# One fused attention, expert and MLP kernel on one Trainium2 core: maxima and halves of the folded weights taken by quarters, and another order of the whole program

## The chip, the cores and the metric

The kernel runs on one core of a Trainium2 chip. The metric is the device time in microseconds (us) of one execution; the median of three runs stands for a kernel. The engines are TensorE (PE, with its weight load PEld), VectorE (DVE), ScalarE (ACT), GpSimd (POOL) and SyncE (SP, which here only issues DMAs). Each works off its own list of instructions in order, and semaphores hold an instruction until its operands are there.

## The reference

Three stages follow one another, for 4 sequences (B) of 576 rows and 512 channels:

```python
attn = softmax(causal(q @ k.T / 8 + decay(f))) @ v         # 8 heads of 64
x    = attn as (B, 576, 512)
# four experts: attention over all rows, then each row keeps its two best
for e in range(4):
    ye = softmax(causal((x @ wq[e]) @ (x @ wk[e]).T / 8)) @ (x @ wv[e]) @ wo[e]
    out += gate[e] * ye                                    # gate: softmax of the two largest of x @ w_gate
# mixer
h = (out.T @ U @ V).T
u = out + h
result = u + relu(u @ w_ch1) @ w_ch2
```

The weights w_ch1 and w_ch2 arrive as 64-bit floats and are turned into 32-bit ones on the chip. The kernel never forms `u` in 512 channels: it keeps the 256 channels of the four heads, folds `wo` into `w_ch1` (512 x 2048 becomes 256 x 2048, the "folded weights"), and later multiplies by `wo` once for the residual.

## The kernel before

Most products are done as three float16 matmuls: each operand is split into a high half (a scaled copy, on ACT) and a low half (the residue, on DVE or POOL), and `TERMS` (line 46) lists the three products that are kept. A split needs a power-of-two scale, and so the largest absolute value of the whole operand: `absmax` (line 329, a DVE reduction), `pow2` (352, over all partitions by one small PE transpose) and `scales` (371).

For each batch b the program runs eight heads of kind 1, written (1, b, h), the projections of their result (`project`, 901, and `values_gates`, 938), four heads of kind 2, (2, b, e), then `mix` (1215), which makes the two halves `z` of the mixer's input, and the MLP: `hidden` (1291; PE tile `hid`, from z and the folded weights), `relu` (1313; tiles g) and `outputs` (1324; tile `acc`, from g and w2). A head is `scores` (553, tile `sp`, or `acc` for 576 columns), `softmax` (581: row minimum on DVE, exponential on ACT, then halves `P`, turned by a DMA transpose into `pt`; some heads are turned on PE instead, `turn_head`, 648), and `pair_pv` (711, the product with V).

The order of the work is written by a planner that runs while the program is built. Every piece above is a thread (`spawn`, 181) with a number from the table `PR` (45); `run` (210) always takes the thread that could start first by the planner's own costs, with `PEN` (39) times its number added as a handicap: a low number goes first. So one number changed in PR can move instructions everywhere.

What is prepared beside the first batch:

- `prep` (1134) issues the loads of U, V, 16 pieces of w_ch1 and 16 of w_ch2, 512 KB each, on SP's queue into three buffers `wd`. `f64_to_f32` (1050) turns a piece into float32: on ACT a scaled copy and a Sign, on DVE a shift and a shift-or, on POOL or DVE a multiply by the sign. Numbers `fold` and `f64_2` of PR go with the pieces of w_ch1 (tile `x`) and w_ch2 (in place in `w2x`).
- `fold` (1110): eight PE matmuls on one piece x and `wtr`, the turned wo, into `hid`; one ACT copy puts the result into `wfr`. The profile shows the eight float32 matmuls of a fold as 16 rows.
- `wf_scaled` (1173) waits for all 16 folds, gives the space of x and wtr to later tiles (`turn`, 1043), takes eight maxima over `wfr`, one scale, and makes eight pairs of halves, in place, one block further down.
- `w2_scaled` (1188) waits for all 16 pieces of w2x, gives the space of `wd` and `sg` to the tiles z and g (line 1190), and makes w2's halves. `w2_done` (1126) takes w2's maxima on ACT or DVE as the planner finds cheaper.
- `hidden` waits once for all halves (event "wf") and then, per batch, for z.

Of the kernel before, what the change touches and what calls it, by code (L numbers as in the profile page):

```python
# [35 lines left out]
WHOLE = 10  # L36
QUEUE = ('act', 'act', 'sp', 'act')
ACTDMA = 100
PEN = 13.823999999999998
WINDOW = 10240 / 3  # L40
WARM = 3300.0
LAG = 100.0
AHEAD = 16
PROJ_EXP = 15
PR = {'load': 3.25, 'low0': -2.0, 'low': 5.75, 'zeros': -2.0, 'scores': 3.25, 'soft0': 1, 'soft2_0': 1.0, 'soft': 5.5, 'soft2_': 9.5, 'pv0': -0.25, 'pv': -0.75, 'pvout0': 2.5, 'pvout': 4.0, 'project0': 3.75, 'project': 0.25, 'vg0': 0.25, 'vg': 4.75, 'out0': 1.75, 'out': 3.0, 'values0': 1.0, 'values': -1.0, 'wall': 5.25, 'prep': 6.0, 'f64': -1.25, 'f64_2': 4.25, 'fold': 2.25, 'wf': 1.25, 'w2': 3.75, 'mix': 0.25, 'relu': 0.75, 'store': 2.75, 'hidden': 6.25, 'outputs': 9.25}
TERMS = ((0, 0), (0, 1), (1, 0))

TURN = {(1, 0): 4, (2, 0): 2}
# [110 lines left out]
class Plan:  # L159
# [21 lines left out]
    def spawn(self, gen, prio=1, t=None):  # L181
        self.seq += 1
        th = {"gen": gen, "t": self.now() if t is None else t, "prio": prio, "seq": self.seq, "last": None}
        self.threads.append(th)
        self.step(th, None)
# [58 lines left out]
def attn_moe_mixer(ctx: ExitStack, tc: tile.TileContext, qk, v, f, wall, wot, wo, w1, w2, u3, v3, out):  # L244
# [7 lines left out]
    spawn = plan.spawn  # L252
# [8 lines left out]
    def mm(out_, lhsT, rhs, start, stop, rate=0.4167, **kw):  # L261
        nc.tensor.matmul(out_, lhsT=lhsT, rhs=rhs, start=start, stop=stop, **kw)  # L262
        small = lhsT.shape[0] <= 64 or size(lhsT) <= 64
        plan.tensor(size(rhs) * rate + 2.5 + (105 if small else 0), size(rhs) * (4 if rate > 1 else 1))
# [48 lines left out]
    def copy_scaled(out_, in_, scale=1.0):  # L313
        act(out_, in_, ACT.Copy, scale=scale)
# [146 lines left out]
    def ev(*name):  # L461
        if name not in E_:
            E_[name] = Event(plan)
        return E_[name]

    def count(n, *name):
        e = ev(*name)
        if name not in counted:
            counted.add(name)
            e.n = n  # L470
        return e
# [571 lines left out]
    def turn(i, *rings):  # L1043

        raw[i].release()
        late = ctx.enter_context(tc.tile_pool(name=f"late{i}", bufs=1, side=SIDES[i]))
        for r in rings:
            r.pool = late
# [61 lines left out]
    def fold(x, c):  # L1110
        yield ev("wtr")
        r = r_hid
        both = yield r
        pp = both[:, :, :128]
        for m in range(2):
            yield "pe"
            for kc in range(4):
                mm(pp[:, m, :], wtr[:, kc, m * 128:(m + 1) * 128], x[:, kc, :], kc == 0, kc == 3, rate=1.8)
        r_x.free(x)
        yield "act"  # L1120
        o = 128 * (c % 4)
        copy_scaled(wfr[:, 1 + c // 4:6 + c // 4:4, o:o + 128], pp)
        r.free(both)
        count(16, "fold").done()

    def w2_done(x, s, c):
        if (yield Any(act=280 + 0.833 * DM, dve=70 + 1.04 * DM)) == "act":
# [6 lines left out]
    def prep():  # L1134
        todo = [(u3.rearrange("p k (n t) -> p k n t", t=2), [128, KB, 96], None, u_done)]
        for c in range(2):
            cs = slice(c * 288, c * 288 + 288)
            todo.append((v3[:, c * 576:(c + 1) * 576].rearrange("p (n t) -> p n t", t=2), [96, 288], None,
                         lambda x, _, cs=cs: v_done(x, cs)))
        ones = [(w1[:, :, c * 256:(c + 1) * 256].rearrange("p k (n t) -> p k n t", t=2), [128, 4, 128], None,  # L1140
                 lambda x, _, c=c: fold(x, c)) for c in range(16)]
        twos = [(w2[:, c, :].rearrange("p (n t) -> p n t", t=2), [128, DM], w2x[:, c + 1, :],
                 lambda x, s, c=c: w2_done(x, s, c), c < 6) for c in [*range(6, NF), *range(6)]]
        todo += ones[:AHEAD]
        for c in range(16):
            todo += ones[AHEAD + c:AHEAD + c + 1] + twos[c:c + 1]
        yield "sp"
        got = dma(wtr, wot)
        spawn(wo_scale(got), PR['prep'])
        yield ev("rows of first")  # L1150
        for src, shape, d, done, *late in todo:
            if len(shape) == 3 and shape[0] == 128 and shape[1] == 4:
                yield ev("aug", 0)
            if d is not None:

                yield ev("aug", B - 1)
                if late[0]:
                    yield ev("wall")
            w = yield r_wd.of(shape + [2], I32, "wd")
            yield QUEUE[2]  # L1160
            spawn(f64_to_f32(w, dma(w, src, queue(2)), shape, d, done), PR['f64' if d is None else 'f64_2'])
# [8 lines left out]
        s_wo[0], _ = scales("won", e, 11)  # L1170
        ev("wo scale").done()

    def wf_scaled():
        yield count(16, "fold")
        yield ev("u")
        yield count(2, "v")
        turn(1, r_ynz, r_th, r_o)
        for i in range(8):
            yield "dve"
            absmax(mxf[:, i:i + 1], wfr[:, 1 + i])  # L1180
        e = yield from pow2("wf", mxf, 8)
        s_wf[0], s_wf[1] = scales("wf", e, 2)
        ev("wf scale").done()
        for i in range(8):
            yield from split(wfs[:, i, 0], wfs[:, i, 1], wfr[:, 1 + i], s_wf[0])
        ev("wf").done()

    def w2_scaled():
        yield count(NF, "w2x")
# [99 lines left out]
    groups = [(b, g) for b in range(B) for g in range((64 * b + 576) // 256)]  # L1289

    def hidden():
        yield ev("wf")
        for b, g in groups:
            yield ev("z", b)
            zt, z0 = ZT[b], g * 256
            for n in range(8):
                r = r_hid if b < B - 1 else r_sp
                hp = yield r.of([128, 2, 256], F32, "hid")
                for fi in range(2):
                    f_ = 2 * n + fi  # L1300
                    fs = slice(f_ % 4 * 128, f_ % 4 * 128 + 128)
                    yield "pe"
                    for kc in range(2):
                        for i, (w_, x_) in enumerate(TERMS):
                            mm(hp[:, fi, :], wfs[:, 4 * kc + f_ // 4, w_, fs], zt[x_][:, kc, z0:z0 + 256], kc + i == 0,
                               kc == 1 and i == 2)
                spawn(relu((b, g, n), r, hp), PR['relu'])
            if (b, g + 1) not in groups:
                count(3 if b < B - 1 else 2, "z free", b).done()
# [163 lines left out]
    spawn(values(0), PR['values0'])  # L1473
    spawn(prep_wall(), PR['wall'])
    spawn(prep(), PR['prep'])
    for b in range(B):
        for p in range(4):
            spawn(pair_pv(1, b, p), PR['pv0' if b == 0 else 'pv'])
        spawn(project(b), PR['project0' if b == 0 else 'project'])
        spawn(values_gates(b), PR['vg0' if b == 0 else 'vg'])  # L1480
        spawn(free_xt(b), 0)
        for p in range(2):
            spawn(pair_pv(2, b, p), PR['pv0' if b == 0 else 'pv'])
        spawn(mix(b), PR['mix'])
        spawn(free_z(b), 0)
# [51 lines left out]
```

## Time and profile before

| | us |
|---|---|
| median of three runs (800.39 to 806.13) | 800.57 |
| the profiled execution | 796.3 |
| its span, first to last instruction | 794.6 |

The profile is of one execution. Its span is 1.7 us shorter than that execution's own time, and that execution is 4.3 us under the median of the runs. The rows that the prediction reads stand in a section of their own below.

### The profile page before, as it was taken

Reading aid. Unit: us, or ns where it says so; the run is one execution under the profiler, and the core shown is the slowest. Engines: PE = TensorE matmul, PEld = TensorE weight load, DVE = VectorE, ACT = ScalarE, POOL = GpSimd, SP = SyncE. Lnnn points to the kernel's source line nnn. Section 1 sums busy time; section 2 is a strip of 40 time slices with the busy share of each in tenths; the row PEclk is TensorE's granted clock in tenths of the full one; section 3 lists DMA queues with packets and bytes.
Section 4 is the critical chain, followed back from the end, with each engine's and each line's share of the span. In section 5 each row is a group of like instructions: output and inputs, shape, how many; then the busy total and the mean of one; then the engine's idle time right before and its main releaser. Section 6 shows DMA issues by size and latency. Waiting matters only on the chain.

```text
span 794.6 us, 15708 instructions
## 1 busy us (share of the span) xinstructions
PE 684.1 (86%) x5720; PEld 480.7 (60%) x5720; DVE 485.6 (61%) x1559; ACT 429.3 (54%) x893; POOL 302.9 (38%) x365
## 2 busy tenths in 40 slices
PE   3777889898655889989969989997999999899996
PEld 2555668686644556756646667565666756555653
DVE  5798985568688884566686637657663572311111
ACT  3677775767586674555656536566562562211121
POOL 4132263234585542247676304666761242000000
PEclk9899999898556999999979999999899999999999
DMA  8546198476589755599999848999976565000000
GB/s 223 128 92 135 45 203 198 136 195 163 144 194 195 135 97 102 109 188 178 221 227 204 134 94 156 179 227 216 199 135 105 121 123 92 27 1 27 1 27 26
DMA packets 210817, 107.28 MB, mean 135 GB/s; under 512 B 172340, under 2 KB 191796, under 8 KB 210708
## 3 DMA queue, kind: packets, MB, share of 16 engines
q1 hardware_dynamic: 190324, 81.28, 52.0%
q0 software_dynamic: 8096, 16.22, 10.3%
q10 hardware_dynamic: 12320, 8.78, 4.8%
q8 instruction: 45, 0.74, 0.4%
q14 instruction: 32, 0.26, 0.1%
HBM read 51.90 MB, written 5.16 MB: 72 GB/s over the span
## 4 chain that ended last, share of the span: by engine, by line
PE 53%; DVE 17%; DMA 12%; ACT 9%; issue 5%; POOL 2%; ACTq 1%; SPq 0%; POOLq 0%; DVEq 0%
PE mm L262 19%; PE acc L262 15%; PE hid L262 12%; DMA pt<-P 10%; PE sp L262 5%; ACT sc L267 3%; DVE sc L273 2%; DVE cols L273 2%; DVE w2x L273 2%; ACT P L267 1%; POOL P L285 1%; DVE pt L273 1%; PE hid L664 1%; DMA YW<-in_qk 1%; ACT pt L267 1%
## 5 line engine op out<-in xcount | busy, mean ns | idle before, releaser
L262 PE MATMUL acc<-w2x,g 128*128 128x512 f16 x768 | 181.4, 381 | 0.0
L285 POOL TENSOR_TENSOR P<-sc,P 128x448 f16<-128x448 f32 (+4 forms) x128 | 102.9, 811 | 149.3 <-ACT P L267 123.6
L262 PEld LDWEIGHTS <-g 128*128 128x128 f16 x864 | 82.3, 98 | 83.7 <-issue 1.9
L267 ACT ACTIVATE sc<-sc,nm 128x576 f32<-128x576 f32 (+4 forms) x195 | 105.7, 558 | 42.9 <-DVE nm L273 40.2
L262 PE MATMUL hid<-z,wfr 128*128 128x256 f16 x864 | 115.5, 283 | 12.8 <-DVE g L273 4.3
L273 DVE SCALAR_TENSOR_TENSOR g<-hid,g 128x512 f16<-128x512 f32 x72 | 49.6, 690 | 119.8 <-ACT g L267 119.7
L262 PEld LDWEIGHTS <-wfr 128*128 128x128 f16 x864 | 84.5, 101 | 39.6 <-issue 11.0
L267 ACT ACTIVATE g<-hid 128x512 f16<-128x512 f32 x72 | 42.6, 592 | 104.9 <-PE acc L262 71.1
L262 PE MATMUL mm<-V,pt 128*128 128x65 f16 (+1 forms) x1992 | 87.4, 205 | 7.7 <-DMA pt<-P 7.1
L267 ACT ACTIVATE P<-sc 64x64 f16<-64x64 f32 (+4 forms) x174 | 74.3, 459 | 30.4 <-DMA pt<-P 27.3
L262 PE MATMUL sp<-X 128*128 128x256 f32 (+1 forms) x132 | 54.5, 420 | 26.1 <-POOL X L285 11.9
L262 PEld LDWEIGHTS <-pt 128*128 128x128 f16 x1872 | 63.1, 99 | 10.1 <-DMA pt<-P 7.6
L273 DVE TENSOR_TENSOR P<-sc,P 128x448 f16<-128x448 f32 (+4 forms) x52 | 42.1, 812 | 25.1 <-ACT P L267 24.6
L262 PEld LDWEIGHTS sp<-X 128*128 128x128 f32 x132 | 29.0, 219 | 40.1 <-DVE nm L273 20.6
L273 DVE CUSTOM_DVE_ANT_0 sc<-sp,mask 128x288 f32<-128x288 f32 (+4 forms) x115 | 48.4, 425 | 7.7 <-POOL P L285 2.9
L285 POOL TENSOR_TENSOR xh<-xn,xh 128x320 f16<-128x320 f32 x30 | 26.6, 888 | 66.3 <-ACT xh L267 65.6
L285 POOL TENSOR_TENSOR x<-x,sg 128x512 f32<-128x512 f32 (+2 forms) x19 | 24.1, 1269 | 71.1 <-ACT sc L267 25.1
L262 PE MATMUL mm<-xt,wall 128*128 128x288 f16 x384 | 51.0, 290 | 0.0
L262 PE MATMUL sp<-Y 68*128 68x256 f32 (+1 forms) x132 | 44.3, 342 | 0.0
L262 PEld LDWEIGHTS <-wall 128*128 128x128 f16 x384 | 38.1, 100 | 9.8
L273 DVE CUSTOM_DVE_ANT_0 sc<-sp,mask,cols 128x192 f32<-128x192 f32 (+4 forms) x80 | 38.1, 487 | 8.9 <-POOL P L285 3.7
L262 PE MATMUL hid<-x,wtr 128*128 128x128 f32 x256 | 35.2, 292 | 2.8 <-POOL xh L285 1.7
(150 smaller groups left out, 1204.0 us busy)
## 6 DMA issues: line engine op xcount, KB each, us to landing
wd<-in_w SPq DMA_DIRECT2D x32, 512.0 KB
Y<-in_qk POOLq DMA_DIRECT2D x22, 288.0 KB, 4.8
R<-in_qk SPq DMA_DIRECT2D x22, 288.0 KB
X<-in_qk POOLq DMA_DIRECT2D x22, 288.0 KB, 5.3
vr<-in_v ACTq DMA_DIRECT2D x16, 320.0 KB
out_dram<-o SPq DMA_DIRECT2D x18, 256.0 KB
Xh<-stg SPq DMA_DIRECT2D x16, 216.0 KB
X<-in_qk POOLq DMA_DIRECT2D x22, 144.0 KB, 4.4
```

The source lines that it names most:

```text
L262: nc.tensor.matmul(out_, lhsT=lhsT, rhs=rhs, start=start, stop=stop, **kw)
L267: nc.scalar.activation(out_, in_, fn, **kw)
L273: getattr(nc.vector, op)(**kw)
L285: getattr(nc.gpsimd, op)(out=out_, **kw)
L664: nc.tensor.transpose(flat[:, 128 * i:128 * i + 128], x[:, 128 * kb:128 * kb + 128], identr)
```

## The change

The rows of `wfr` are laid out by quarters of the 2048 hidden channels (both blocks of 128 input channels of a quarter side by side). The maxima of a quarter wait only for its four folds ("folds", q), the halves report each quarter by itself ("wf", q), and `hidden` waits for the quarter that it uses. The scale is still one for all eight blocks, so every pair of halves stands behind all eight maxima. The release of space is split off into `raw_free`, a thread of its own. Most of the numbers in PR are different, and PEN is a quarter larger; of those that belong to the weights, `fold` goes from 2.25 to 1.75 and `f64_2` from 4.25 to 5.25, and `project0` from 3.75 to 2.25.

```diff
-PEN = 13.823999999999998
+PEN = 17.279999999999998
...
@@ def fold
-        copy_scaled(wfr[:, 1 + c // 4:6 + c // 4:4, o:o + 128], pp)
+        copy_scaled(wfr[:, 1 + 2 * (c // 4):3 + 2 * (c // 4), o:o + 128], pp)
         r.free(both)
         count(16, "fold").done()
+        count(4, "folds", c // 4).done()
...
-    def wf_scaled():
+    def raw_free():
         yield count(16, "fold")
         yield ev("u")
         yield count(2, "v")
         turn(1, r_ynz, r_th, r_o)
+
+    def wf_scaled():
         for i in range(8):
+            yield count(4, "folds", i // 2)
             yield "dve"
             absmax(mxf[:, i:i + 1], wfr[:, 1 + i])
...
         for i in range(8):
             yield from split(wfs[:, i, 0], wfs[:, i, 1], wfr[:, 1 + i], s_wf[0])
-        ev("wf").done()
+            if i % 2:
+                ev("wf", i // 2).done()
...
@@ def hidden
-        yield ev("wf")
         for b, g in groups:
...
             for n in range(8):
+                yield ev("wf", n // 2)
...
-                            mm(hp[:, fi, :], wfs[:, 4 * kc + f_ // 4, w_, fs], zt[x_][:, kc, z0:z0 + 256], kc + i == 0,
+                            mm(hp[:, fi, :], wfs[:, 2 * (f_ // 4) + kc, w_, fs], zt[x_][:, kc, z0:z0 + 256], kc + i == 0,
...
+    spawn(raw_free(), 0)
```

On PE, where the scores of the first heads of kind 2 stand (`Xh`), the program before reads as follows; `hid<-x,wtr` is a fold, in two parts of four matmuls, and `mm<-identr,sc` turns a head on PE.

```order
L262 LDWEIGHTS Xh
L262 MATMUL sp<-Xh 128x448
L262 MATMUL hid<-x,wtr 128x128 x4
L664 MATMUL mm<-identr,sc_96 128x128
L664 MATMUL mm<-identr,sc_97 128x128 x2
L262 MATMUL hid<-x,wtr 128x128 x4
```

At the same scores the changed program reads as follows; `mm<-identr,cols` is the transpose in a scale, here that of the folded weights, and `mm<-wall,xt` belongs to `values_gates`.

```order
L262 MATMUL mm<-wall_81,xt 128x260
L262 MATMUL mm<-identr,cols 128x128
L664 MATMUL hid<-identr,sc_98 128x128 x3
L262 LDWEIGHTS Xh
L262 MATMUL sp<-Xh 128x448
```

Before, 11 of the 16 folds and 66 of the 96 projection matmuls (`mm<-xt,wall`) of batch 0 stand in front of the first scores with Xh; now all 16 and all 96 do.

On DVE, the maxima of wfr stand before among the scores of the last two heads of kind 2 (`sc<-sp,mask,cols`; `ISA nm` reads out a minimum) and right in front of conversions of w2.

```order
L273 TENSOR_REDUCE cols<-wfr 128x1
L273 ISA sc_100,nm<-sp,mask,nm,cols 128x288
L273 ISA nm 128x1
L273 TENSOR_REDUCE cols<-wfr 128x1
L273 TENSOR_SCALAR w2x<-w2x 128x512
L273 TENSOR_REDUCE cols<-cols 128x1
L273 TENSOR_TENSOR rr<-rr,wq 128x5 x2
L273 SCALAR_TENSOR_TENSOR w2x<-wd,w2x 128x512
```

The first two maxima now stand among the conversions of w_ch1 (x), while the last heads of kind 1 of the first nine are still scored.

```order
L273 ISA sp,nm<-sp,mask 128x448
L273 ISA nm 128x1
L273 TENSOR_REDUCE cols<-wfr 128x1
L273 TENSOR_SCALAR x<-x 128x512
L273 TENSOR_REDUCE cols<-wfr 128x1
L273 SCALAR_TENSOR_TENSOR x<-wd,x 128x512
L273 TENSOR_SCALAR nm<-nm 128x1
L273 ISA acc,nm<-acc,mask 128x288
L273 ISA nm 128x1
```

The other six follow in pairs, all in front of the first score of kind 2.

On DVE, the low halves of wfr stand before between conversions of w2 and heads of batch 1.

```order
L273 SCALAR_TENSOR_TENSOR wfr<-wfr,cols 128x512
L273 TENSOR_TENSOR xn<-mm,rr 128x320
L273 TENSOR_SCALAR w2x<-w2x 128x512
L273 TENSOR_SCALAR nm<-nm 128x1 x2
L273 SCALAR_TENSOR_TENSOR wfr<-wfr,cols 128x512
L273 SCALAR_TENSOR_TENSOR w2x<-wd,w2x 128x512
L273 TENSOR_SCALAR w2x<-w2x 128x512
L273 SCALAR_TENSOR_TENSOR wfr<-wfr,cols 128x512
```

They now stand among the scores of kind 2, in front of the gates.

```order
L273 ISA sc_96,nm<-sp,mask,cols 64x64
L273 ISA nm 64x1
L273 ISA sc_97,nm<-sp,mask,cols 128x192
L273 ISA nm 128x1
L273 SCALAR_TENSOR_TENSOR wfr<-wfr,cols 128x512
L273 SCALAR_TENSOR_TENSOR w2x<-wd,w2x 128x512
L273 ISA sc_98,nm<-sp,mask,cols 128x320
```

All eight are now in front of the gates, and four conversions of w2 stand ahead of the last of them; before, they began after the gates had been used, with eight conversions of w2 ahead of the first of them and eleven ahead of the last. Between the use of the gates (`rr<-rr,wq`) and the halves of z, DVE's row holds 11 conversions of w2 and all eight low halves before, and 9 conversions and no half now.

## Rows read from the trace of the kernel before

**Rows 1.** The page, part 1: busy us (share of the span) xinstructions of each engine.
```profile
span 794.6 us, 15708 instructions
...
PE 684.1 (86%) x5720; PEld 480.7 (60%) x5720; DVE 485.6 (61%) x1559; ACT 429.3 (54%) x893; POOL 302.9 (38%) x365
```

**Rows 2.** Windows: stretch, length, each engine's busy us (instructions), PE clock, DMA share, GB/s.
```profile
72.00:94.60 22.60, 16.80 (x156) 11.84 (x156) 20.04 (x67) 16.00 (x33) 3.64 (x4) 0.92 0.42 85
94.60:140.30 45.70, 40.31 (x443) 35.78 (x443) 32.52 (x90) 30.85 (x68) 23.46 (x24) 0.96 0.82 184
140.30:191.80 51.50, 45.16 (x330) 36.47 (x328) 33.76 (x103) 36.61 (x82) 15.13 (x15) 0.93 0.62 165
191.80:255.70 63.90, 40.12 (x235) 35.14 (x235) 52.55 (x127) 44.47 (x96) 41.24 (x43) 0.55 0.78 174
255.70:316.10 60.40, 52.22 (x443) 33.74 (x441) 44.58 (x117) 37.98 (x73) 25.66 (x26) 0.94 0.61 117
316.10:682.00 365.90, 340.10 (x3153) 234.17 (x3153) 226.50 (x852) 198.83 (x425) 173.35 (x211) 0.97 0.88 158
682.00:794.60 112.60, 103.39 (x612) 60.67 (x612) 19.03 (x33) 20.58 (x33) 0.00 (x0) 0.97 0.05 19
```

**Rows 3.** PE's timeline, 70 to 330 us: start, us, line, out<-in, count, [idle before].
```profile
98.23 2.03 PE L262 MATMUL hid<-x,wtr 128*128 128x128 f32 x16
...
136.37 1.27 PE L262 MATMUL mm<-xt,wall 128*128 128x288 f16 x9
...
140.25 1.15 PE L262 MATMUL sp<-Xh 128*128 128x64 f16 x8
...
174.77 6.81 PE L262 MATMUL mm<-V,pt 128*128 128x65 f32 x60
...
202.30 6.50 PE L262 MATMUL mm<-V,pt 128*128 128x65 f32 x30
...
222.53 0.58 PE L262 MATMUL sp<-X 128*128 128x256 f32 x1 [10.96 <-POOL X L285]
...
225.38 3.40 PE L262 MATMUL mm<-y,u 128*96 128x256 f16 x15
```

**Rows 4.** DVE's groups by form: count | busy us, mean ns | idle before.
```profile
L273 DVE TENSOR_SCALAR w2x<-w2x 128x512 int32<-128x512 int32 x16 | 13.0, 813 | 3.1 <-ACT w2x L267 3.1
...
L273 DVE SCALAR_TENSOR_TENSOR w2x<-wd,w2x 128x512 int32<-128x512 int32 x16 | 12.0, 747 | 0.3
L273 DVE SCALAR_TENSOR_TENSOR x<-wd,x 128x512 int32<-128x512 int32 x16 | 11.9, 746 | 0.2
...
L273 DVE SCALAR_TENSOR_TENSOR wfr<-wfr,cols 128x512 f16<-128x512 f32 x8 | 8.7, 1085 | 0.5 <-ACT wfr L267 0.5
...
L273 DVE TENSOR_SCALAR x<-x 128x512 int32<-128x512 int32 x16 | 8.0, 500 | 7.6 <-ACT x L267 7.4
...
L273 DVE TENSOR_REDUCE cols<-wfr 128x1 f32<-128x512 f32 x8 | 5.3, 682 | 0.0
```

**Rows 5.** DVE's timeline, 184 to 262 us.
```profile
191.81 0.24 DVE L273 TENSOR_TENSOR rr<-rr,wq 128x5 f32<-128x5 f32 x2
...
224.94 0.89 DVE L273 SCALAR_TENSOR_TENSOR wfr<-wfr,cols 128x512 f16<-128x512 f32 x1
...
237.73 0.16 DVE L273 RECIPROCAL cols<-cols 128x1 f32<-128x1 f32 x1
...
255.74 1.42 DVE L273 SCALAR_TENSOR_TENSOR z<-y,cols,z 128x1152 f16<-128x1152 f32 x1
```

**Rows 6.** ACT's timeline, 222 to 260 us.
```profile
254.16 0.19 ACT L267 ACTIVATION_READ_ACCUMULATOR sg<-w2x 128x1 f32 x1
254.38 1.26 ACT L267 ACTIVATE z<-y,cols 128x1152 f16<-128x1152 f32 x1
```

**Rows 7.** Tile wfr on DVE: ns min/median/max, first and last start us.
```profile
L273 DVE TENSOR_REDUCE cols<-wfr x8: 676/682/687, 177.7 to 190.8; 128x1 f32<-128x512 f32 x8
...
L273 DVE SCALAR_TENSOR_TENSOR wfr<-wfr,cols x8: 745/864/1747, 204.0 to 224.9; 128x512 f16<-128x512 f32 x8
```

More of the change, by code (lines that the diff above doesn't have):

```diff
@@ L44 @@
 PROJ_EXP = 15
-PR = {'load': 3.25, 'low0': -2.0, 'low': 5.75, 'zeros': -2.0, 'scores': 3.25, 'soft0': 1, 'soft2_0': 1.0, 'soft': 5.5, 'soft2_': 9.5, 'pv0': -0.25, 'pv': -0.75, 'pvout0': 2.5, 'pvout': 4.0, 'project0': 3.75, 'project': 0.25, 'vg0': 0.25, 'vg': 4.75, 'out0': 1.75, 'out': 3.0, 'values0': 1.0, 'values': -1.0, 'wall': 5.25, 'prep': 6.0, 'f64': -1.25, 'f64_2': 4.25, 'fold': 2.25, 'wf': 1.25, 'w2': 3.75, 'mix': 0.25, 'relu': 0.75, 'store': 2.75, 'hidden': 6.25, 'outputs': 9.25}
+PR = {'load': 4.25, 'low0': -1.0, 'low': 5.75, 'zeros': -2.0, 'scores': 3.25, 'soft0': 1.5, 'soft2_0': 0.75, 'soft': 5.75, 'soft2_': 9.5, 'pv0': 0.0, 'pv': -1.0, 'pvout0': 2.75, 'pvout': 7.0, 'project0': 2.25, 'project': -2.0, 'vg0': 0.25, 'vg': 5.75, 'out0': 1.5, 'out': 2.0, 'values0': 1.0, 'values': -0.5, 'wall': 5.25, 'prep': 6.0, 'f64': -1.25, 'f64_2': 5.25, 'fold': 1.75, 'wf': 1.25, 'w2': 3.75, 'mix': 0.25, 'relu': -0.25, 'store': 1.0, 'hidden': 4.25, 'outputs': 9.0}
 TERMS = ((0, 0), (0, 1), (1, 0))
```

## The prediction

> **What bounds the kernel now.** Read the page's first part first: PE is busy for 684.1 of 794.6 us [rows 1], so it bounds the kernel wherever it has work. The windows then say where it has none. From 316.1 us, where batch 1's projections begin, PE is busy for 340.1 of 365.9 us and then for 103.4 of 112.6, at a clock of 0.97: there the time is PE's, and its work is the same after the change [rows 2]. Before that the stages differ. From 72 to 94.6 us DVE has 20.0 of 22.6 us; up to 140.3, where folds and projections share PE, PE has 40.3 of 45.7; up to 191.8, the stage of the heads of kind 2, PE has 45.2 of 51.5 and DVE only 33.8. Then comes the poor stage, 191.8 to 255.7: PE is busy for 40.1 of 63.9 us and that at a granted clock of 0.55, thus almost wholly at 1.2 GHz, while DVE has 52.6, ACT 44.5 and POOL 41.2 us [rows 2]. No engine is full there, but each stands in order behind the others.
>
> Next read the timelines for what ends this stage. It ends when DVE makes batch 0's z at 255.74 [rows 5]; only then can `hidden` fill PE. The last low half of wfr stands at 224.94, 31 us earlier [rows 5], so the wait for the halves is not what ends last. The scale of z is known at 237.9 (its reciprocal) [rows 5], but ACT starts z at 254.38, behind the last maximum of w2 at 254.16 [rows 6]: z's tiles lie where wd and sg lay (line 1190), so z needs every conversion of w2 to be done. Sixteen conversions, the eight halves and eight maxima of wfr, and heads of batch 1 all press into DVE, ACT and POOL there.
>
> **The change part by part.** The folds' work is not removed; it changes its place. I take four steps, at the boundaries of the windows, and count in each what stands between the same two instructions on DVE (first score of kind 2; first use of the gates; low half of z; first projection of batch 1), each at its mean from the trace before; of a sum the large items are named, the rest are single instructions of up to 1.1 us.
>
> Step 1, to the first scores of kind 2 (72 to 140.3). PE gets five more folds in front of them, 5 x 2.03 = 10.2 us, and 30 more projection matmuls, 30 x 1.27/9 = 4.2 [rows 3]: 14.4 us. DVE gets 8 maxima of 0.68 (5.5), the conversions of four pieces x (4 x (0.50 + 0.75) = 5.0), one conversion of w2 (0.81 + 0.75 = 1.6) and small ones: +13.8 [rows 4]. These lie beside idle time: in the two windows DVE has 2.6 + 13.2 = 15.7 us of it and PE 5.8 + 5.4 = 11.2 [rows 2]. If PE used all of its gaps, the step would cost 14.4 - 11.2 = 3 us; if it kept its share of 57.1/68.3, 14.4/0.836 = 17. I take +10: a fold is a chain over ACT, DVE, POOL and PE, and the gaps that the folds left before are of the same kind.
>
> Step 2, the heads of kind 2 (140.3 to 191.8). The same 14.4 us leave PE. DVE loses the maxima and the four pieces (10.5) and gets eight halves of 1.09 (8.7) [rows 4] and three maxima of w2 from ACT at 0.68: about nothing in sum. ACT loses the pieces' copies and gets the eight high halves. PE was the fullest engine, so the stage shrinks by 14.4 at most, and by nothing if the heads' own chain (score, exponential, turn, copy, product) sets its length. I take -8, a little over half.
>
> Step 3, from the gates to z (191.8 to 255.7). DVE loses the eight halves (8.7) and two conversions of w2 (3.1) [rows 4], and with one head of batch 1 that now stands behind z some four more: -15.5 in sum. POOL's and ACT's rows lose with it. At DVE's share of 52.6/63.9 [rows 2] the stage would shrink by 15.5/0.82 = 19; if the conversions' chain (load, ACT, DVE, POOL, ACT) sets the pace, at 63.9/11 = 5.8 us each, nine in place of eleven save 11.6, and less if they share that time with the heads: 5 is my lower end. What is then late next is the chain of the heads: product, transpose, `mix`, z. It holds one wait that shows that it can be shorter: PE stood 10.96 us for POOL's X until 222.53, and `mix` came behind it at 225.38 [rows 3]. I take -14.
>
> Step 4, z to the projections of batch 1 (255.7 to 316.1). The head that was put behind z, and a few subtractions that went from POOL to DVE, give DVE +5.2. DVE had 44.6 of 60.4 us and PE 52.2 [rows 2]. Between 0 (hidden beside PE) and +7 (at DVE's share) I take +3.
>
> The rest is no step. Waiting by quarters for the halves costs and gives nothing, since z comes 31 us behind them [rows 5]; the cover is 31 us deep, and step 3 takes some 14 of it while the halves move ahead by more. PE's work behind 316.1 is the same, and DVE, with 226.5 of 365.9 us [rows 2], hides seven subtractions that moved to it. The table PR also shuffles the later batches, which I put at 0 with an end of 4 us on either side (of PE's 25.8 us of idle time there a sixth).
>
> Sum: +10 - 8 - 14 + 3 = -9 us. The profiled execution of 796.3 us (span 794.6 and 1.7 around it) would become 787.3. The median of the runs is 4.3 us longer than it, and I carry that over: 800.6 - 9 = 791.6 us.
>
> A row that bears on step 3: the halves took 745 to 1747 ns, the maxima 676 to 687, of the same 512 elements [rows 7]; POOL was busy for 41.2 of 63.9 us there and for 15.1 of 51.5 in the stage that the halves go to [rows 2]. The Trainium skill (SBUF — State Buffer, "Who interferes with whom") says that a DVE instruction with two inputs in SBUF and a GpSimd instruction that reads SBUF exclude each other for a whole instruction, and that reductions never do; the rows agree. By it the halves would come near 745 ns beside a quieter POOL, and 8 x (1085 - 745) = 2.7 us more would be gained; by the mean of the rows, nothing. I leave it out of the sum.
>
> **The rivals.** First, both waits in front of z go: PE's 10.96 us [rows 3] and ACT's 16.5 us between the scale of z and z (237.9 to 254.4) [rows 5, 6], because conversions of w2 end with `mix`. Then step 3 brings 25, not 14: 800.6 + 10 - 8 - 25 + 3 = 780.6. For it: in the new order the last conversion of w2 stands just in front of z's scale. Against it: nine conversions are still left at the gates.
>
> Second, the work only moves: step 1 costs 15, step 2 saves 8, step 3 saves 10, since the conversions and not the halves set its pace, and step 4 takes 3 back. Sum 0, 800.6 us. For it: DVE's count up to 316 us is no smaller than before. In that case the change doesn't do what it says, for its quarters would start nothing earlier.
>
> Third, slower: TensorE's clock. Step 2 leaves PE some 31 us of work in a stage of 43, and in step 3 before, where PE was as thin, the granted clock was 0.55, against 0.93 in this stage [rows 2]. At 1.2 GHz the float32 products of a head take 6.50 us for 30 rows, as against 6.81 for 60 [rows 3]. If the clock falls at the start of step 2, PE's 31 us become 62, and PE itself sets the stage: 62 - 51.5 = +10.5 in place of -8. Sum +10 + 10.5 - 14 + 3 = +9.5: 810. It decides from a granted clock of about 0.7 in that stage, where the work is as long as the stage. The Trainium skill (TensorE: Matmul & The Clock Gate, Part 1) says that the clock follows PE's recent activity, with 1.2 GHz as the idle state; the rows of both stages agree with that. Against the rival: heads, values and turns still come close together there.
>
> **How the numbers follow.** Forecast, 785 to 798: 0.45. First rival 0.22, second 0.20, third 0.13. A measurement of this kernel tells about 1% (8 us) from no change. Under 792.6 lie the first rival and six tenths of the forecast: 0.22 + 0.27 = 0.49. Within 1% lie the rest of the forecast and the second: 0.38. Slower is the third: 0.13. The range leaves out the ends of the first and the third: 778 to 808.
>
> **What would show it.** First scores of kind 2 at 147 to 155 us; gates used at 190 to 198; z at 238 to 248 with no low half of wfr within 40 us ahead of it; projections of batch 1 at 303 to 311; from there to the end the same 478 us within 4. The forecast is wrong if z comes no earlier than 252, if the granted clock between the scores of kind 2 and the gates is under 0.7, or if what is won by 310 us is lost behind it.

## The result, and the profile after

The changed kernel took 781.84 us (median of 780.02, 781.84, 784.19) against 800.57: a ratio of 0.9755, 95% interval 0.9711 to 0.9798. The forecast of 791.6 had the sign and half the size; 781.8 lies inside its range. Each ratio here leaves out executions more than 1.5% above the fastest of the same kernel, while the medians take all. A second measurement, beside other kernels of this study, gave 782.67, ratio 0.9788 (0.9733 to 0.9843). So 17 to 19 us were gained where 9 were forecast.

The page of the profiled execution (780.02 us), as [rows 1]:

```profile
span 778.3 us, 15717 instructions
...
PE 669.4 (86%) x5720; PEld 469.1 (60%) x5720; DVE 506.7 (65%) x1575; ACT 423.7 (54%) x882; POOL 299.5 (38%) x357
```

Read this row against [rows 1] before anything else. The span fell by 16.3 us. PE's busy time fell by 14.7 (684.1 to 669.4) with the same 5720 matmuls, and its idle time by only 1.6 (110.5 to 108.9). The granted clock, as a mean over the span, rose from 0.927 to 0.949; busy time times clock is 634 us before and 635 after. So the same matmul work was done at a higher clock. That is bookkeeping and not yet a cause: a second profiled execution of the changed kernel (span 780.0 us) has PE busy for 675.8 us at 0.940, which makes 8.3 of 14.6 us, and the kernel with the code alone, below, has 668.9 us and is not faster.

The windows of after at its own boundaries (first scores of kind 2 at 153.05, gates at 191.7, z at 232.6, end of batch 1's projections at 311.2, last z at 666.4), as [rows 2]:

```profile
core 0: us, PE busy (x) PEld busy (x) DVE busy (x) ACT busy (x) POOL busy (x), PEclk, DMA share, GB/s
72.00:153.05 81.05, 67.95 (x704) 58.87 (x702) 65.94 (x173) 55.21 (x118) 33.40 (x32) 0.98 0.68 169
153.05:191.70 38.65, 28.85 (x192) 22.03 (x190) 34.18 (x99) 31.82 (x67) 12.19 (x11) 0.87 0.55 136
191.70:232.60 40.90, 28.11 (x210) 24.71 (x209) 36.24 (x100) 31.85 (x73) 29.55 (x33) 0.75 1.03 222
232.60:311.20 78.60, 69.94 (x609) 48.63 (x608) 56.52 (x162) 45.82 (x89) 31.47 (x34) 0.93 0.67 130
311.20:666.40 355.20, 326.49 (x3044) 222.44 (x3041) 237.54 (x834) 194.94 (x416) 172.48 (x206) 0.97 0.89 159
666.40:778.30 111.90, 102.99 (x612) 60.41 (x612) 18.92 (x32) 20.27 (x33) 0.00 (x0) 0.97 0.05 19
```

The stage from the gates to z has shrunk from 63.9 to 40.9 us, and its clock has risen from 0.55 to 0.75. PE is busy there for 28.1 us instead of 40.1, and idle for 12.8 instead of 23.8. PE's timeline of after, as [rows 3], shows where:

```profile
178.71 5.25 PE L262 MATMUL mm<-V,pt 128*128 128x65 f32 x30 [3.38 <-DVE lg L273]
...
191.70 6.81 PE L262 MATMUL mm<-V,pt 128*128 128x65 f32 x60
...
202.81 3.46 PE L262 MATMUL mm<-V,pt 128*128 128x65 f32 x30
...
212.26 0.58 PE L262 MATMUL sp<-X 128*128 128x256 f32 x1 [5.99 <-POOL X L285]
...
215.52 2.93 PE L262 MATMUL mm<-y,u 128*96 128x256 f16 x15
```

The last float32 products of kind 2 take 3.46 us a head (60 rows are two heads); the row at 202.30 in [rows 3] has 6.50, and so has the head ahead of it in before:

```profile
193.55 6.50 PE L262 MATMUL mm<-V,pt 128*128 128x65 f32 x30
```

The wait for X is 5.99 us, not 10.96. DVE's timeline of after, as [rows 5]:

```profile
177.70 0.74 DVE L273 SCALAR_TENSOR_TENSOR wfr<-wfr,cols 128x512 f16<-128x512 f32 x1
...
191.75 0.39 DVE L273 TENSOR_TENSOR rr<-rr,wq 128x5 f32<-128x5 f32 x1 [1.06 <-DMA wq<-lg]
...
230.85 0.16 DVE L273 RECIPROCAL cols<-cols 128x1 f32<-128x1 f32 x1
...
232.64 1.41 DVE L273 SCALAR_TENSOR_TENSOR z<-y,cols,z 128x1152 f16<-128x1152 f32 x1
```

The last low half stands 14 us ahead of the gates. ACT's timeline, as [rows 6]:

```profile
230.33 0.19 ACT L267 ACTIVATION_READ_ACCUMULATOR sg<-w2x 128x1 f32 x1
231.11 1.26 ACT L267 ACTIVATE z<-y,cols 128x1152 f16<-128x1152 f32 x1 [0.59 <-DVE cols L273]
```

The last maximum of w2 and the scale of z now come within 0.5 us of each other. That is the state the first rival described: before, ACT began z 16.5 us behind the scale.

### The profile page after: what moved, and what is told of

Same layout as the page of the kernel before. It is cut to its first block, busy times and chain, and to the rows that moved or that the text cites. A ratio compares the mean times of both kernels' runs of the same rounds, so it can differ in the third digit from the quotient of the medians.

```text
span 778.3 us, 15717 instructions
## 1 busy us (share of the span) xinstructions
PE 669.4 (86%) x5720; PEld 469.1 (60%) x5720; DVE 506.7 (65%) x1575; ACT 423.7 (54%) x882; POOL 299.5 (38%) x357
## 4 chain that ended last, share of the span: by engine, by line
PE 37%; DMA 11%; DVE 5%; ACT 3%; issue 3%; POOL 2%; SPq 1%; ACTq 0%; DVEq 0%; POOLq 0%
PE mm L262 13%; PE acc L262 13%; DMA pt<-P 8%; PE hid L262 8%; PE sp L262 4%; DVE sc L273 2%; ACT P L267 1%; POOL P L285 1%; DMA R<-in_qk 1%; ACT sc L267 1%; DMA vr<-in_v 1%; DVE P L273 1%; DVE rr L273 1%; DMA xt<-xh 1%; DVE g L273 0%
## 5 line engine op out<-in xcount | busy, mean ns | idle before, releaser
L285 POOL TENSOR_TENSOR P<-sc,P 128x448 f16<-128x448 f32 (+4 forms) x132 | 110.1, 841 | 166.2 <-ACT P L267 124.1
L262 PE MATMUL hid<-z,wfr 128*128 128x256 f16 x864 | 113.8, 281 | 9.9 <-DVE g L273 5.6
L267 ACT ACTIVATE P<-sc 128x192 f16<-128x192 f32 (+4 forms) x172 | 73.9, 459 | 26.1 <-DMA pt<-P 22.3
L262 PE MATMUL mm<-V,pt 128*128 128x65 f16 (+1 forms) x1992 | 82.4, 202 | 6.2 <-DVE lg L273 3.4
L262 PE MATMUL sp<-X 128*128 128x256 f32 (+1 forms) x132 | 52.5, 406 | 28.3 <-POOL X L285 20.3
L273 DVE TENSOR_TENSOR P<-sc,P 128x448 f16<-128x448 f32 (+4 forms) x48 | 46.0, 963 | 19.4 <-ACT P L267 19.2
L273 DVE CUSTOM_DVE_ANT_0 sc<-sp,mask 128x192 f32<-128x192 f32 (+4 forms) x115 | 47.7, 425 | 6.4 <-PE sp L262 4.6
L285 POOL TENSOR_TENSOR xh<-xn,xh 128x320 f16<-128x320 f32 x28 | 24.0, 856 | 68.5 <-ACT xh L267 53.1
L262 PEld LDWEIGHTS <-wall 128*128 128x128 f16 x384 | 37.6, 98 | 10.4 <-issue 0.7
L262 PE MATMUL hid<-x,wtr 128*128 128x128 f32 x256 | 33.1, 282 | 9.0 <-ACT wfr L267 3.2
```

What stands on the lines that cost most here:

```text
L267: nc.scalar.activation(out_, in_, fn, **kw)
L273: getattr(nc.vector, op)(**kw)
L285: getattr(nc.gpsimd, op)(out=out_, **kw)
```

## The experiments

All times are medians and all ratios are against before, measured on the same chip. Stages are read from the profiled executions, one for each kernel, and some of these lie well off their kernel's median (code alone is the fastest of ten, 7.5 us under it; halves late is the slowest of ten, 6.6 us over it). Up to their first scores of kind 2, executions of one order differ by some 6 us (before and three kernels with its order: 137.2, 137.8, 140.2 and 143.6 us). So within a trace only lengths between boundaries are compared.

The theory from the two traces had two parts: TensorE's clock in the float32 products, and the halves and conversions that left the stage. The rivals were that only the planner's numbers matter, or only the conversions of w2.

### Code and numbers apart

The code of after with the old table:

```diff
-PEN = 17.28
-PR = {... 'project0': 2.25, 'f64_2': 5.25, 'fold': 1.75, ...}
+PEN = 13.824
+PR = {... 'project0': 3.75, 'f64_2': 4.25, 'fold': 2.25, ...}
```

> The quarters of wfr with the numbers (PR and PEN) of before. Theory 'pieces' (the quarters themselves give the gain, because maxima and halves can leave the stage in front of z): at least half of the 18.7 us, so 782 to 791 us, with z at 246 us or earlier. Rival 'numbers' (the gain is that of the planner's new numbers, which put folds, conversions and heads in another order): within 1% of before, 793 to 808 us, z at 250 us or later; in this kernel's order 27 softmax instructions of batch 1 stand on VectorE between the first use of the gates and z, as against 18 before and 15 after, which speaks for the rival.

The code of before with PEN and PR of after:

> The code of before with the numbers of after; the maxima wait for all 16 folds, the halves come after them. Theory 'pieces': the numbers alone give less than half, 792 to 803 us. Rival 'numbers': 780 to 791 us, z at 240 us or earlier. If both parts are needed, neither this kernel nor the one with the code alone comes under 791 us.

Measured: code alone 805.33 us, ratio 1.0044 (1.0004 to 1.0083); numbers alone 793.38, 0.9910 (0.9872 to 0.9947). Neither comes under 791, so both are needed: the numbers alone bring 7 us, and the code alone brings none. The page of the kernel with the code alone:

```profile
span 796.0 us, 15738 instructions
...
PE 668.9 (84%) x5720; PEld 469.1 (59%) x5720; DVE 495.2 (62%) x1562; ACT 427.2 (54%) x891; POOL 301.7 (38%) x363
```

It has the busy PE time of after (668.9, against 669.4), but 127.1 us of idle time, 18 more. In this execution PE's busy time is down as far as in after, and what PE waits for takes it back; so a fall of PE's busy time says nothing by itself of a gain. Its z came 81.6 us behind the first use of the gates, which stands at 175.66 there.

### Is it the conversions of w2?

The last two of 16 pieces left out of before, first in an unchanged order (their instructions are not issued, their place in the plan is kept), then out of the plan too:

```diff
-for c in [*range(6, NF), *range(6)]]
+for c in [*range(6, NF), *range(4)]]      (second kernel)
```

> Before, in an unchanged order, with the conversion of the last two of 16 pieces of w2 left out (their load, copies, shifts, the multiplication by the sign; their maxima stay, on a constant). Theory 'z waits for the conversions' space': the last conversion left starts at 235.1 us on ACT, so ACT begins z at 239 to 241 in place of 254.4, 13 to 15 us earlier, and the time falls by 9 to 15 us, to 786 to 792. Rival 'work only' (z stands where it does because VectorE, ACT and POOL have that much to do in front of it): the two pieces are 2 x 2.0 us on VectorE, 2 x 1.3 on ACT and 2 x 1.3 on POOL, and z moves by no more than 5 us.

> Before, with the same two conversions of w2 left out as in the run that left them out in an unchanged order (there the time did not move), but here left out of the plan too (with their maxima), so that the order is drawn anew: z stands some 26 rows earlier on VectorE, with 13 softmax rows of batch 1 between the gates and z in place of 18. Two fills of 0.3 us stand behind z. Theory 'place in the order' (z is late because ACT's and VectorE's rows of batch 1's heads stand in front of it and wait there for a transposed copy): z begins on ACT at 236 to 244 us and the time falls to 784 to 792. Rival 'work' (VectorE, ACT and POOL have that much to do): as with the unchanged order, z at 250 or later and 797 to 805 us.

Measured: 801.97 us, 1.0021 (0.9985 to 1.0057), z 67.5 us behind the gates, no earlier than before. Then 812.49 us, 1.0152 (1.0085 to 1.0219), z 51.1 us behind them. The chain of waits of the first kernel says why less work brought nothing:

```profile
239.04 0.54 POOL P L289
239.60 13.24 DMA pt<-P
252.92 1.15 ACT P L269 x2
254.07 0.62 ACT sg L269 x2
254.72 1.26 ACT z L269
```

The same stretch of the chain in before:

```profile
242.49 1.54 POOL P L285
244.06 8.19 DMA pt<-P
252.33 0.69 ACT P L267
```

z stands in ACT's order behind a copy into P for a head of batch 1. That copy waits until an earlier P has been read by its transposed copy. With two pieces fewer the same rows waited longer on ACT, 8.42 us instead of 2.63; first before, then the kernel with two pieces fewer:

```profile
252.33 1.15 ACT L267 ACTIVATE P<-sc 128x576 f16<-128x576 f32 x2 [2.63 <-DMA pt<-P]
252.92 1.15 ACT L269 ACTIVATE P<-sc 128x576 f16<-128x576 f32 x2 [8.42 <-DMA pt<-P]
```

So the prediction's reading (z waits for the end of the conversions) named the row just ahead of z and not what ended late. Drawn anew, the order put z ahead of those rows, and z came early as expected. The time did not follow, against what was expected: it was lost behind z, as its window from the end of batch 1's projections to the last z shows, 377.7 us against 354.0 in before and 355.2 in after:

```profile
322.70:700.40 377.70, 335.63 (x3044) 228.98 (x3041) 225.13 (x822) 195.97 (x420) 175.70 (x214) 0.94 0.83 150
```

### Is it the clock?

Four kernels in unchanged orders. In before, 7 of the 15 products of each of the last two heads left out; in after, the same heads' products done twice; in before and in after, matmuls that nobody reads (fillers) put into PE's waits:

```diff
+if (kind, b, p) == (2, 0, 1) and kb >= (1, 1, 2, 2, 2)[blk]:
+    ...
+    continue
...
+for kb in range(blk + 1 if (kind, b, p) == (2, 0, 1) else 0):
+    ...
+    nc.tensor.matmul(pv[:, blk, :], ..., start=blk + kb == 0, stop=kb == blk, ...)
...
+def fill(n):
+    for _ in range(n if FILL else 0):
+        nc.tensor.matmul(FILL[0][:, 0, :], lhsT=wallx[0][:, 0, 0:128], rhs=wallx[0][:, 0, 0:512], start=True, stop=True)
```

> Before, in an unchanged order, with 7 of 15 float32 products left out in each of the last two heads of kind 2 of batch 0 (those at 193.6 and 202.3 us that took 6.50 us per head at the granted clock of 0.50). TensorE then needs 3.5 us for each, about what it needs after the change at the full clock; 6.1 us go. Theory 'one chain' (products, next scores, POOL's subtractions for X, SyncE's queue, last load of w2, z): X at 222.5 comes 6 us earlier, z at 249 to 251 in place of 255.7, and the time falls by 4 to 7 us to 794 to 797. Rival 'conversions' (ACT, VectorE and POOL set the end of the conversions of w2 by their own work, whatever TensorE does): z moves by less than 2 us and the time by less than 3.

> After, in an unchanged order, with the 15 float32 products of each of the last two heads of kind 2 of batch 0 done twice (the second pass starts each sum anew). They took 3.46 us per head at the full clock; twice that, 6.9, is about what the same heads took in before at a granted clock of 0.50 (6.50 each). Theory 'one chain' (products, next scores, X, transposed copies, z): z begins on ACT at 236 to 239 us in place of 231.1 and the time rises by 5 to 8 us over after. Rival 'covered' (TensorE waits 5.99 us for X behind these products anyhow, and the conversions of w2 end with z): z moves by less than 2 us, the time by less than 3.

> Before, in an unchanged order, with matmuls that nobody reads (128x512 f16, into the two PSUM banks that stand empty there) put into TensorE's waits: two ahead of each of the 20 groups of transposes of kind 2's heads, 24 ahead of the scores that wait 10.96 us for X, 5 ahead of the products with vst. Theory 'clock' (the gain in the stage from the gates to z is mostly TensorE's granted clock: 0.55 before, 0.75 after): the clock from 192 to 202 us holds, the float32 products take 3.5 to 5 us in place of 6.50 per head, X and z come 3 to 6 us earlier, and the time falls by 3 to 8 us (0.990 to 0.996 of before, as with half the products left out). Rival 'work' (the fillers find no gap that is free, or the products are not what sets z): the time stays within 2 us of before or rises.

> After, in an unchanged order, with the same fillers: one ahead of each group of transposes, 8 ahead of the first float32 product (TensorE waits 3.38 us there, and the product took 5.25 us), 14 ahead of the scores that wait 5.99 us for X, 10 ahead of the products with vst (4.44 us of wait). Theory 'clock': the first product takes 3.5 us, the products with vst 2 us in place of 3.2; but the last maximum of w2 stood at 230.33, 0.5 us ahead of the scale of z, so z can come only some 1 to 2 us earlier and the time is 778 to 782, against after in the same call. Rival: the fillers stand in the way of what they precede (28 fillers at the low level are 12 us), and the time rises by 2 us or more.

> The changed kernel once more, beside the two with fillers and before, on one chip. Both theories expect 0.971 to 0.980 of before, as measured; it is the yardstick for the filled one.

Measured: products halved in before 792.58 us, 0.9891 (0.9848 to 0.9934), z 60.6 us behind the gates instead of 63.9, though some 6 us of PE's work are gone there. Products doubled in after 786.79, 0.9840 (0.9749 to 0.9931), 4 to 5 us over after by the medians (the intervals overlap), z 46.9 us behind the gates instead of 40.9. Of the 6.9 us put on PE in after, 6.0 reach z (4.8 against the second execution of after); of the 6 us taken off in before, 3.3 do.

Before with fillers (77 matmuls; the transposes stand in 24 groups, not 20): 794.53 us, 0.9931 (0.9894 to 0.9969). No instruction of any other engine differs. Its PE timeline, and its window from the gates to z:

```profile
197.28 3.46 PE L262 MATMUL mm<-V,pt 128*128 128x65 f32 x30
...
205.48 5.22 PE L262 MATMUL mm<-V,pt 128*128 128x65 f32 x30 [0.97 <-DVE cols L273]
...
224.43 0.58 PE L262 MATMUL sp<-X 128*128 128x256 f32 x1 [5.48 <-POOL X L285]
```

```profile
195.60:257.00 61.40, 42.44 (x272) 32.71 (x270) 54.05 (x128) 44.95 (x97) 40.99 (x43) 0.76 0.84 183
```

One head's products are back at 3.46 us and the other's at 5.22. The clock is a cause of its own: held up by useless work, it takes 5.5 us (2.5 to 8.5) off before, about three tenths of the gain. But it is not the larger part of this stage's gain by itself, as the theory had it: at a granted clock of 0.76, the level of after, z still came 61.3 us behind the gates, 2.6 earlier than in before and less than the 3 to 6 expected; where the rest of the 5.5 us lies, this one execution does not show. Of the 4.3 us that the products saved, 1.9 are left when X's scores begin: behind the products the chain of waits goes over halves of wfr and conversions of w2 on DVE, here as in before:

```profile
216.05 1.67 DVE wfr L273
217.72 0.95 DVE w2x L273
219.21 1.35 DVE wfr L273
```

After with fillers took 782.36 us, beside 782.67 without them. Its first product took 3.56 us, but the last maximum of w2 and the scale of z still came together (233.47 and 233.98), and z came 42.1 us behind the gates with them and without.

What PE did before the clock fell, in slices of before:

```profile
core 0: us, PE busy (x), PEclk, DMA share, GB/s
184.00:188.00 4.00, 3.47 (x25) 1.00 0.85 192
188.00:192.00 4.00, 1.99 (x11) 0.91 0.72 146
192.00:196.00 4.00, 3.35 (x16) 0.50 0.46 131
```

and of after:

```profile
176.00:180.00 4.00, 1.29 (x12) 1.00 0.78 133
180.00:184.00 4.00, 4.00 (x22) 0.54 0.21 83
184.00:188.00 4.00, 2.75 (x11) 0.50 0.72 200
188.00:192.00 4.00, 3.61 (x19) 0.68 0.64 154
192.00:196.00 4.00, 4.00 (x38) 1.00 0.75 197
```

and of the kernel in which the halves follow the gates, which comes next:

```profile
184.00:188.00 4.00, 1.53 (x8) 1.00 0.77 197
188.00:192.00 4.00, 2.60 (x11) 0.51 0.65 157
192.00:196.00 4.00, 4.00 (x21) 0.50 0.68 231
```

In all three the granted clock went to 1.2 GHz (0.50) behind a slice in which PE had little to do, 1.99, 1.29 and 1.53 of 4 us. In after this happened 12 us earlier, at the first head; the clock was back at 2.4 GHz when the next two came. The Trainium skill (TensorE: Matmul & The Clock Gate, Part 1) makes the clock follow PE's recent activity, with 1.2 GHz as the idle state; the falls in the slices and the fillers agree. The slices do not show what brings the clock back: with the halves late PE is counted as busy in every slice from 192 to 212 us, all of it float32 matmuls, and the clock stays at 0.50. They do show that the halves are not what made it fall. It fell by 192 us in before and by 188 with the halves late, and the first low half stands at 204.0 and 193.0.

### What the halves cost where they stood

After with one wait more, so that the halves follow the gates; and the same order with products left out:

```diff
+yield ev("gate", 0)
 for i in range(8):
     yield from split(wfs[:, i, 0], ...)
```

> After, with one wait more: the halves of wfr begin only when the gates of batch 0 are there (the maxima stay early). The planner then puts all eight behind the first use of the gates, as in before; else the order up to z differs little (z stands at row 521 of VectorE, after at 519). Theory 'halves' (in before they stood on the path to z, on VectorE's rows at 210 to 224 us, and their leaving is the larger part of what the stage gained): the stage from the gates to z grows by 8 to 13 us and the time goes to 789 to 796. Rival 'clock and order' (the stage is short because TensorE's clock holds in the products and fewer heads stand ahead of z): the stage grows by less than 4 us, the time stays at 780 to 786.

> The kernel with the halves held behind the gates, in an unchanged order, with 7 of 15 float32 products left out in each of the last three heads of kind 2 of batch 0. There these products ran at a granted clock of 0.50, 12.90 us for two heads and 6.62 for one, 19.5 in all as against 10.27 after the change; 7/15 of 19.5 is 9.1 us. Theory 'the halves cost twice' (once as VectorE's and ACT's own work, some 9 us, and once because TensorE falls to the low level behind them, 9 us): the stage from the gates to z shrinks from 59 to 50 to 52 us, and the time goes from 803.9 to 794 to 798. Rival 'halves alone' (their rows and the conversions set z, the products run beside them): z moves by less than 3 us and the time stays at 800 to 806.

Measured: 803.90 us, 1.0064 (1.0020 to 1.0107), all of the gain gone by one wait, and more than the 789 to 796 expected; the stage from the gates to z is 59.0 us, 18.1 longer than in after, and the stretch from the end of batch 1's projections to the last z is 11.2 longer. With 7 of the 15 products of each of the last three heads left out the stage is 49.9, and the time 797.85, 0.9943 (0.9892 to 0.9995). PE's timeline of the first kernel:

```profile
192.17 12.90 PE L262 MATMUL mm<-V,pt 128*128 128x65 f32 x60
...
206.68 6.62 PE L262 MATMUL mm<-V,pt 128*128 128x65 f32 x30
```

and its low halves by form on DVE:

```profile
L273 DVE SCALAR_TENSOR_TENSOR wfr<-wfr,cols 128x512 f16<-128x512 f32 x8 | 10.4, 1298 | 0.1
```

The wait cost twice. The products took 9.3 us more than in after (12.90 + 6.62 against 6.81 + 3.46), since with the halves moved the clock fell just ahead of the gates; leaving about as much work out (9.1 us) brought z 9.1 us nearer. The other 9.0 of the 18.1 us remain for the halves, whose rows are 10.4 us on DVE here; that part is a remainder and was not tried by itself.

### How much hangs on this one order

Before with PEN alone changed; after with four numbers set back, which leaves the order up to z as it is; after with the numbers of the later heads set back; after with PEN at 16.8:

```diff
-PEN = 13.824
+PEN = 17.28                                                      (before)
-'relu': -0.25, 'store': 1.0, 'hidden': 4.25, 'outputs': 9.0
+'relu': 0.75, 'store': 2.75, 'hidden': 6.25, 'outputs': 9.25      (after)
-'pv': -1.0, 'pvout': 7.0, 'project': -2.0, 'vg': 5.75, 'out': 2.0, 'values': -0.5
+'pv': -0.75, 'pvout': 4.0, 'project': 0.25, 'vg': 4.75, 'out': 3.0, 'values': -1.0    (after)
-PEN = 17.28
+PEN = 16.8                                                       (after)
```

> Before, with PEN alone changed to the value of after (13.824 to 17.28); no quarters, PR as before. The planner then puts 17 folds in place of 12 ahead of the first scores of kind 2, seven conversions of w2 in place of five ahead of the gates, and 15 softmax rows of batch 1 in place of 18 between the gates and z (after: 18, 7 and 15). Theory 'place in the order' (the gain is what stands where, whichever edit brings it about): z 238 to 246 us, the time 782 to 792. Rival 'pieces' (without quarters the early maxima and halves are not to be had): 794 to 806 us.

> After, with the numbers of relu, store, hidden and outputs as in before (0.75, 2.75, 6.25, 9.25). The order is the same up to z of batch 0; only behind it does it change (some 790 rows on TensorE). Theory 'the numbers were fitted to this order' (in five runs with any other mixture of code and numbers the stretch from the end of batch 1's projections to the last z took 366 to 378 us, in before 354 and in after 355): the stretch grows to 361 or more and the time goes to 788 to 803. Rival 'these numbers do nothing that can be seen': the stretch stays within 4 us of 355 and the time at 778 to 786.

> After, with the numbers of pv, pvout, project, vg, out and values for the later batches as in before. Halves and maxima stand where after has them, seven conversions of w2 stand ahead of the gates as in after, but one head of batch 1 more (20 softmax rows in place of 15) stands between the gates and z. Theory 'place in the order': z comes 5 to 10 us later than in after (stage 46 to 51 us in place of 41) and the time goes to 787 to 803, the larger part of it behind z if the numbers were fitted to one order. Rival 'halves only' (with the halves out of the stage a head more is hidden): the stage stays under 44 us and the time under 787.

> After, with PEN at 16.8 in place of 17.28. The planner then puts four conversions of w2 in place of seven ahead of the gates, all eight halves behind or just ahead of the gates, and 22 softmax rows of batch 1 in place of 15 between the gates and z. Theory 'the gain hangs on this one order': the time goes to 792 to 812 us though quarters and numbers are all there. Rival 'quarters carry it' (a planner that may start early finds some early place): within 1% of after, 774 to 790.

Measured, in this order: 826.39 us, 1.0301 (1.0215 to 1.0388); 788.41, 0.9873 (0.9787 to 0.9958); 810.47, 1.0081 (1.0023 to 1.0139); 792.46, 0.9895 (0.9853 to 0.9936). The first was a plain miss: few rows of batch 1 ahead of z did not make it fast. With one head more z came 14.1 us later than in after, where 5 to 10 were expected. The window from the end of batch 1's projections to the last z, of after with four numbers set back:

```profile
313.90:678.20 364.30, 332.04 (x3043) 226.59 (x3041) 231.14 (x833) 195.85 (x419) 169.56 (x204) 0.95 0.87 155
```

The stages, as lengths between the same instructions (us, worked out from the traces; the gates are their first use, the projections those of batch 1):

| kernel | first scores to gates | gates to z | z to end of projections | to last z | of it PE idle |
|---|---|---|---|---|---|
| before | 51.6 | 63.9 | 72.6 | 354.0 | 26.1 |
| after | 38.7 | 40.9 | 78.6 | 355.2 | 28.7 |
| after, measured again | 38.9 | 42.1 | 75.5 | 357.8 | 28.2 |
| before with fillers | 52.0 | 61.3 | 73.7 | 353.7 | 26.5 |
| code alone | 35.8 | 81.6 | 57.2 | 370.9 | 33.6 |
| numbers alone | 35.3 | 59.8 | 65.8 | 367.8 | 34.1 |
| halves late | 34.9 | 59.0 | 78.6 | 366.4 | 35.9 |
| two pieces fewer, new order | 50.2 | 51.1 | 81.2 | 377.7 | 42.1 |
| four numbers back | 38.6 | 42.0 | 79.4 | 364.3 | 32.3 |
| one head more | 38.5 | 55.0 | 69.5 | 377.2 | 42.7 |
| PEN alone | 48.4 | 51.2 | 83.0 | 371.4 | 41.8 |
| PEN at 16.8 | 16.4 | 73.0 | 65.8 | 369.4 | 37.2 |

Every other drawing of the order needs 363 to 378 us for the late stretch, where before, after and the kernels with their orders need 353 to 360. Four numbers, with the same order up to z, go with 7 to 9 us more there; the kernel's median is 6 to 7 us over after's, with intervals that overlap (up to 0.9798 and from 0.9787), and its profiled execution is the slowest of four. This suggests that a good part of the PR numbers that moved do not make the gain but keep it; it is not shown clear of noise. Which waits make the other late stretches longer was not traced.

## Why the prediction was right or wrong

**Step 1 (forecast +10, bounds 3 to 17).** Right: the first scores of kind 2 moved from 140.25 to 153.05, +12.8 (up to there executions of one order differ by some 6 us).

**Step 2 (-8, bounds 0 to -14.4).** Right in kind, at the far end of its bounds: 51.6 became 38.7 us, -12.9. The gates stand at 191.75, where they stood before (191.81), inside the forecast's 190 to 198.

**Step 3 (-14, bounds -5 to -19): the step that failed.** It came to -23.0, outside its bounds. The sum was made from DVE's rows (halves, two conversions, a head), scaled by DVE's share of 52.6 in 63.9 us. TensorE's work stands in it at nothing. [rows 2] showed a clock of 0.55 in this stage, and the prediction used it only against the change, as the third rival. In place of the sum the runs put three parts, in the order in which they were taken off:

- 4.9 us between before (63.9) and after with the halves late (59.0), which has seven conversions of w2 ahead of the gates in place of five; this part was not tried by itself;
- 9.1 us with TensorE's time in the float32 products (59.0 to 49.9), which is the missing term;
- 9.0 us (49.9 to 40.9) as the remainder, put down here to the halves; their rows in the sum are 8.7.

The parts hang on each other. With the halves and eleven conversions still in the stage the same rise of the clock brought z only 2.6 us nearer (before with fillers), and leaving half of the products out only 3.3. And the halves' leaving is not, in itself, what gave the clock back: the clock falls ahead of the gates, by what PE waits for there, and the new order moved that fall to an earlier head. That this happened was no part of the forecast.

**What ends the stage.** The prediction held that the end of the conversions gates z. The run with two fewer shows that in before it was ACT's order: the last maximum and z stood behind a copy into P that waited for a transposed copy. z came at 232.64, earlier than the 238 to 248 forecast. Two readings of this stage were loose too: five of the sixteen conversions and all eight maxima of wfr (177.7 to 190.8, [rows 7]) stand ahead of the gates in before, and not in it; the sum used the right eleven.

**Step 4 (+3, bounds 0 to +7) and the rest (0, ends 4).** Both came out inside their bounds. z to the first projection, the prediction's boundary, grew by 3.8 us; z to the end of the projections grew by 6.0 us, and from there to the end of the span the time went from 466.3 to 467.1, +0.8. Batch 1's projections began at 297.05 (24 of 96) and 302.24, earlier than the 303 to 311 forecast. The rest came out right for a reason that the prediction did not have: it took the table for a shuffle that averages out, while in the profiled executions every other order drawn took 7 to 23 us more there. On that count the forecast was lucky.

**Sum.** +12.8 - 12.9 - 23.0 + 6.0 + 0.8 = -16.3, the change of the span; -9 was forecast. Of the seven missing, nine are step 3's and five step 2's, less three of step 1, three of step 4 and one of the rest (step 4 taken to the end of the projections).

**The rivals.** The first (both waits ahead of z go, 780.6 us) was nearest, 1.2 us from the median, and its 25 us for step 3 were right within 2. Of its two waits ACT's 16.5 us between the scale and z went, and of PE's 10.96 us for X 5.0 did. But it credited the conversions, where TensorE's time and the halves make up 18.1 of the 23.0 us, so that its number came so near is in part luck. The second fell. The third named the right quantity with the wrong sign: from the first scores to the gates the clock was 0.87 where 0.93 had been, above the 0.7 from which it was to decide, and behind the gates it rose.

**The halves' remark** held in direction: they took 850 ns in the mean after (POOL busy for 12.19 of 38.65 us of that stage), 1085 before ([rows 4]; 41.24 of 63.90) and 1298 with the halves late (30.90 of 59.00), so POOL's share alone does not order them. DVE's row by form in after:

```profile
L273 DVE SCALAR_TENSOR_TENSOR wfr<-wfr,cols 128x512 f16<-128x512 f32 x8 | 6.8, 850 | 1.0 <-ACT wfr L267 1.0
```

That is 1.9 us less than before, of the 2.7 left out of the sum.

## What to carry to other kernels

In a stage with a low granted clock, price TensorE's work on the path at both levels (here 6.50 and 3.46 us a head), and look for what TensorE waits for ahead of that stage, since the clock fell there and not where the moved work stood. Busy time times clock, much the same in two kernels, tells how the work was clocked and not what caused a gain: code alone had after's busy time and none of its gain. Before calling a row the bound, look at what stands ahead of it in its engine's order: leaving that row's work out changed nothing here. Two causes on one path can be worth little one by one: the clock alone was 2.6 us of the stage in before, and 9.1 in the new order. Where a planner draws the order, judge a change by the late stretch too.

## What the hardware showed that was not expected

Matmuls that nobody reads, put into TensorE's waits, made before 5.5 us faster, though they stood ahead of work on the path: the products behind them went from 6.50 to 3.46 and 5.22 us a head. In after, where the clock was up for the later heads, 56 such fillers brought 0.3 us, which is nothing.

With the halves late, float32 matmuls had TensorE busy in every slice from 192 to 212 us, and the granted clock was 0.50 throughout.

A transposed copy of P to pt, 8.19 us on the chain of before, took 13.24 us on the chain of the kernel that had less to convert and two loads fewer. Why was not traced.
